# Attention and squared-ReLU FFN on one core: scaling the next pair's q behind the visit's exponentials at the end of a unit

## The chip, the cores and the metric

The kernel runs on one core of one Trainium2 chip. Times are device microseconds of that core, as a median of runs; the profile adds one execution in detail. Lower is better. Engine names: PE is TensorE, DVE is VectorE, ACT is ScalarE, POOL is GpSimd and SP is SyncE, which here only issues DMAs.

## The reference

An attention block with normalized q and k is followed by a feed-forward block, all in float32:

```python
def rmsnorm(x, g):
    return x / np.sqrt(np.mean(x * x, axis=-1, keepdims=True) + 1e-06) * g
# q, k, v: (8, 12, 448, 64); g_q, g_k: (64,)
q_n, k_n = rmsnorm(q, g_q), rmsnorm(k, g_k)
scores = 1 / np.sqrt(64) * np.matmul(q_n, k_n.transpose(0, 1, 3, 2))
scores = scores - scores.max(-1, keepdims=True)
attn = np.exp(scores); attn = attn / (attn.sum(-1, keepdims=True) + 1e-09)
x = np.matmul(attn, v)            # -> (8*448, 12*64) = (3584, 768)
h = np.maximum(x @ w_in, 0)       # w_in: (768, 2048)
out = h * h @ w_out               # w_out: (2048, 768)
```

## The kernel before

**Pairs and visits.** The 96 heads are taken two at a time: 48 pairs, numbered i = 0 to 47, six to a batch element. A pair's q and k are turned so that the head dimension lies on the partitions: two heads of 64 fill 128 partitions, in tiles `qT` and `kT` of 128 x 448. In a visit of pair i its scores are multiplied on TensorE (`score`, L435 and L446), and their exponentials are taken on ACT into tiles `wT` (`weigh`, L454). Between them the attention of the pair before, i - 1, is multiplied (`attend`, with `attend_halves` at L550 and `attend_both` at L571). For i > 24, `whole(i)`, a pair has one visit, `visit_whole`; earlier ones have two. A whole visit goes through three slots of keys: attention of i - 1, scores of i, exponentials of i. At an odd i the PSUM banks of the scores are used in turn, so that the scores of the second slot need a bank which the first slot's exponentials have emptied. At the end of the visit `join_halves` copies two banks on ACT (L561, L562).

**Units and their streams.** The FFN is computed for two batch elements at a time, in four units u = 0 to 3. It is a generator, `ffn(u)`: TensorE multiplies with pre-combined forms of the weights (L986 in unit 0 and L1042 later for the first product, L1251 for the second), and ACT, DVE and POOL move and combine the results. `run(until)` takes steps of this stream up to a point given in costs. Between steps it runs small pieces of work from lists: `tasks`, `pool_tasks`, a `plan` and `transfers`. Twelve pairs' visits are spread over a unit. Where a unit ends (`x == unit`), `drain()` finishes the stream and empties the lists, the next unit's stream is set up, and then the visit follows: no FFN step lies between the drained work and the visit.

**Order.** The order of instructions on every engine is that in which the program issues them, by hand[...]. Nearly all DMAs are issued from SP, in one order too.

**Turning q and k.** For later pairs, `load_blocks` brings q and k in blocks of 32, and `turn_blocks(i, x)` transposes them on DVE (L367). For q (x = 0) it then multiplies `qT` in place on ACT by the 128 factors `g`, which hold g_q * g_k / 8 (L369). Before a whole visit i, tasks for turning k and then q of pair i + 1 are put into `tasks`; most are run between steps of the stream, the rest in `drain()`.

**Other lines named below.** L1039 and L1031 copy a bank of the first product on ACT, and L1027 adds on DVE. L1345 and L1272 add products to the output rows on DVE. L719 is a subtraction that builds a combined form of x (DVE or POOL). L204 and L219 normalize q on POOL; L326 is any DMA that goes through the transfer list: q and k from memory, the normalized q to memory (`q_rows`), and its blocks back. L377 and L384 load v. L892 loads pieces of the first weights (`in_sb`) into a ring, L902 the second weights (`out_sb`), and L1350 stores output rows. `leave(i)` gives up a pair's tiles once its attention is finished.

Of the kernel before, what the change touches and what calls it, by code (L numbers as in the profile page):

```python
# [225 lines left out]
def program(ctx, tc, rows, v, g, wide, ones, moe_w_in, moe_w_out, out, shift):  # L226
# [40 lines left out]
    values, turned, through = {}, {}, {}  # L267
# [9 lines left out]
    def whole(i):  # L277
        return i > 2 * 2 * NPAIR
# [30 lines left out]
    def room_for_blocks(i, x):  # L309
        return rows.room(i)[:, x].rearrange("p g h d -> p (g h d)")[:, ds(i % 2 * S, S)]  # L310
# [17 lines left out]
    def ensure(*key):  # L328

        while any(some[0] == key for some in transfers):  # L330
            follow_transfers(1)
# [32 lines left out]
    def turn_blocks(i, x):  # L364
        ensure("blocks", i, x)
        dst = att.tile([P, S], F32, name="qT" if x == 0 else "kT")
        nc.vector.transpose(dst, room_for_blocks(i, x))  # L367
        if x == 0:
            nc.scalar.mul(dst, dst, g)  # L369
        turned[i, x] = dst  # L370

    def load_v(i):
        b, c = pairs[i]
# [85 lines left out]
    def additions(i):  # L459

        order = [NJ, 2] if i % 2 else [2, NJ]
        for m in [1] + order:
            for e in range(2):
                pool_tasks.append(lambda m=m, e=e: add_up(i, e, m))

    def add_up(i, e, m):
        if m == 1:
            sums[i, e] = new_sum(i)
            left = weights[(i, 0), e]
        else:  # L470
            left = sums[i, e]
        some = ds(i % 2 * LASTS, LASTS) if m == NJ else ds(0, P)
        nc.gpsimd.tensor_tensor(  # L473
            out=sums[i, e][some], in0=left[some], in1=weights[key_of(i, m), e][some], op=ALU.add
        )
        if joint(i) and i % 2 and m == NJ:
            del weights[key_of(i, m), e]
# [217 lines left out]

    def leave(i):
        b, c = pairs[i]
        for x in range(2):
            del turned[i, x]
        del values[i]  # L700
        if b == 1:
            begin_forms(c)
        elif b > 1:
            settle(b, c)
# [16 lines left out]
    def settle(b, c):  # L721

        u = b // 2
        if u - 1 not in through_with and (b % 2 * NPAIR + c) < 8:
            away[b, c] = dram.tile([P, S], F32, name="x_rows", tag="x_rows", bufs=8)
            unsaved[b, c] = xts.pop((b, c))
            later.append([4, lambda: save(b, c)])
        arriving.append([4, (b, c)])
# [5 lines left out]
    def arrive(all_=False):  # L734

        for some in arriving:
            some[0] -= 1
        while arriving and (all_ or arriving[0][0] <= 0):
            here.add(arriving.popleft()[1])
# [101 lines left out]
    def follow_plan(most):  # L841

        while plan and most:
            tiles, x, step = plan[0]
            if tiles > free.get(max(through_with), 0) or not here.issuperset(x):
                break
            plan.popleft()
            if step is not None:
                step()
            most = most - 1 if step else 0  # L850

    def begin_forms(c):

        if c < NK:
            b11, b12, t1 = xts.pop((0, c)), xts.pop((1, c)), new_x()
            less(nc.vector, t1, b12, b11)()
            forms[0, c] = {"11": b11, "T1": t1, "T3": b12}
            return
        c -= NK
        b21, b22, t2, t4 = xts.pop((0, c + NK)), xts.pop((1, c + NK)), new_x(), new_x()  # L860
        some = forms[0, c]
        less(nc.vector, t2, b22, some["T1"])()
        less(nc.gpsimd, some["T3"], b22, some["T3"])()
        less(nc.gpsimd, t4, t2, b21)()
        some.update({"21": b21, "22": b22, "T2": t2, "T4": t4})
# [750 lines left out]
    def run_all():  # L1616
        before = set(held)
        held.clear()
        while tasks or pool_tasks:
            run_tasks(len(tasks) + len(pool_tasks))  # L1620
        if not first:
            follow_transfers(len(transfers))
        held.update(before)

    def drain():
        for _ in stream:
            pass
        while tasks or pool_tasks:
            run_all()
        arrive(True)  # L1630
        while any(some is MARK for some in plan):
            before = len(plan)
            follow_plan(1)
            assert len(plan) < before
# [10 lines left out]
    def load_qk(i):  # L1645
        if i <= last:
            rows.load(i, transfers_of("qk", i))
# [24 lines left out]
    def attend_all(i):  # L1672
        slots = range(NJ + 1)
        attend(i, slots)
        add_weights(i, slots)
        forget(i, slots)
        take_sums(i)
        invert(i)
        finish(i)
# [90 lines left out]
            tasks.append(lambda: load_blocks(i, 1))  # L1770

    def visit_whole(i):
        late = [some for some in tasks if getattr(some, "args", None) == (i,)]
        for some in late:
            tasks.remove(some)
        run_all()
        if shift:
            attend_all(i - 1)
            if i <= last:
                weigh_slots(i, 1)  # L1780
        else:
            if i % 2 == 0:
                both_denominators(i - 2)
            for n in range(NJ):
                attend(i - 1, (n,))
                forget(i - 1, (n,))
                if i <= last:
                    score(i, n)
                    weigh(i, n)
                while n == 1 and i % 2 == 0 and late:  # L1790
                    late.pop(0)()
            if i % 2:
                attend(i - 1, (NJ,))
                forget(i - 1, (NJ,))
            join_halves(i - 1)
            if i % 2 == 0:
                tasks.append(lambda: invert_both(i - 2))
                if i <= last:
                    score(i, NJ)
                    weigh(i, NJ)  # L1800
            if i <= last:
                additions(i)
        tasks.extendleft(reversed(late))
        if late:
            tasks.extendleft([gap] * 3)
        if shift or i % 2:
            prepare(i + 3)
        else:
            tasks.append(lambda: tasks.append(lambda: prepare(i + 3, 0)))
        if i <= last:  # L1810
            tasks.appendleft(lambda: load_v(i))
# [7 lines left out]
    with tc.manual_schedule(engines=ENGINES):  # L1819
        if shift:  # L1820
            rows.scale(0, 1, nc.gpsimd)
        turn(0, 1)
        turn(0, 0)
        for x in range(2):
            rows.normalize_first(1, x, new_acc()[:, 0 : 4 * P])
        if shift:
            rows.scale(1, 1, nc.gpsimd)
        for i in range(len(pairs) + 1):
            for n in range(1 if whole(i) else VISITS):
                at = i * VISITS + n - VISITS - unit  # L1830
                if at < 0:
                    visit_alone(i, n)
                    continue
                u, x = divmod(at, unit)
                if x == 0:
                    u, x = u - 1, unit
                run(place(u, x - (1 if whole(i - 1) else 0.5)))
                if i < last:
                    if whole(i) and not shift:
                        tasks.append(partial(lambda i: turn_blocks(i + 1, 1), i))  # L1840
                        tasks.append(partial(lambda i: turn_blocks(i + 1, 0), i))
                        tasks.append(partial(lambda i: load_qk(i + 4), i))
                    else:
                        for some in (1, 0) if whole(i) else (1 - n,):
                            turn_among(i + 1, some)
                        if n or whole(i):
                            tasks.append(lambda i=i: load_qk(i + 4))
                    if n and first and x > 1 and not shift:
                        denominators(i - 1)
                run(place(u, x))  # L1850
                if x == unit:
                    drain()
                    stream, spent, first = ffn(u + 1), 0, u < 0
                    if shift:
                        run(COST if first else LATER)
                    elif first:
                        run(COST_IN + 1)
                slowly = x < unit
                if whole(i):
                    visit_whole(i)  # L1860
                else:
                    visit_among(i, n)
        run(LATER)
        drain()
        assert not transfers
        for _ in ffn(B // 2 - 1):
            follow_loads()
            follow_plan(1)
# [29 lines left out]
```

## Time and profile before

| | |
|---|---|
| median of 3 runs | 1392.92 us (1391.83 to 1393.26) |
| profiled execution: its own time | 1394.38 us |
| profiled execution: span from first to last instruction | 1392.6 us |
| busy share of the span: PE, DVE, ACT, POOL | 98%, 58%, 44%, 57% |
| PE's granted clock, mean | 0.998 of full speed |
| DMA moved | 233.36 MB, mean 168 GB/s |
| L369, the multiply of q: count, mean | 34, 665 ns |
| L454, the exponentials into wT: count, mean | 288, 631 ns |

The page gives for each engine the time in which it was busy and, for each group of instructions, the idle time in front of them with what ended it. In the timeline a row is a run of like instructions: start and duration in us, engine, line, operation, output<-input, the count, and in brackets the idle time before it and its releaser. PEld is the loading of weights, which overlaps the matmuls; SPq are the DMA issues of SP. The chain of waits starts from the last instruction and follows back what released each step.

### The profile page before, as it was taken

Reading aid. Unit: us, or ns where it says so; the run is one execution under the profiler, and the core shown is the slowest. Engines: PE = TensorE matmul, PEld = TensorE weight load, DVE = VectorE, ACT = ScalarE, POOL = GpSimd, SP = SyncE. Lnnn points to the kernel's source line nnn. Section 1 sums busy time; section 2 is a strip of 40 time slices with the busy share of each in tenths; the row PEclk is TensorE's granted clock in tenths of the full one; section 3 lists DMA queues with packets and bytes.
Section 4 is the critical chain, followed back from the end, with each engine's and each line's share of the span. In section 5 each row is a group of like instructions: output and inputs, shape, how many; then the busy total and the mean of one; then the engine's idle time right before and its main releaser. Section 6 shows DMA issues by size and latency. Waiting matters only on the chain.

```text
span 1392.6 us, 19474 instructions
## 1 busy us (share of the span) xinstructions
PE 1363.3 (98%) x6320; PEld 845.7 (61%) x6320; DVE 807.2 (58%) x1635; ACT 608.3 (44%) x1118; POOL 789.6 (57%) x794
## 2 busy tenths in 40 slices
PE   7999999999999999999999999999999999999997
PEld 3333444444444466676758586676768677868684
DVE  4786545867758755555556755455546642445444
ACT  6885477757666244353434244442434032202020
POOL 5668664746656868576667877566745630303030
PEclk9999999999999999999999999999999999999999
DMA  5566746968769875664739475755527442424223
GB/s 147 149 168 169 203 117 159 264 179 219 233 155 284 231 215 162 187 173 141 204 86 279 140 225 149 211 153 176 146 86 239 142 165 103 135 90 149 78 90 100
DMA packets 385588, 233.36 MB, mean 168 GB/s; under 512 B 272452, under 2 KB 354244, under 8 KB 381380
## 3 DMA queue, kind: packets, MB, share of 16 engines
q1 hardware_dynamic: 385184, 231.95, 57.7%
q8 instruction: 52, 0.85, 0.3%
q14 instruction: 60, 0.49, 0.1%
q10 hardware_dynamic: 292, 0.07, 0.0%
HBM read 174.59 MB, written 57.34 MB: 167 GB/s over the span
## 4 chain that ended last, share of the span: by engine, by line
PE 81%; POOL 4%; DVE 4%; DMA 3%; issue 3%; SPq 2%; ACT 2%; POOLq 0%; ACTq 0%; DVEq 0%
PE bank L1251 30%; PE bank L1042 20%; PE bank L986 8%; PE bank L446 5%; PE bank L536 5%; PE bank L550 4%; PE bank L435 4%; PE bank L1165 2%; POOL sum L473 2%; PE bank L585 1%; DMA qk<-in_k_dram 1%; PE bank L611 1%; SPq L326 1%; SPq L318 1%; PE bank L571 1%
## 5 line engine op out<-in xcount | busy, mean ns | idle before, releaser
L1042 PE MATMUL bank<-xT,in_sb 128*128 128x224 f32 x1344 | 289.3, 354 | 2.9 <-ACT part L1031 2.3
L1251 PE MATMUL bank<-out_sb,hid 128*128 128x384 f32 x768 | 272.5, 488 | 2.2 <-POOL out_sb L1514 1.4
L1345 DVE TENSOR_TENSOR acc<-acc,bank 128x384 f32<-128x384 f32 x312 | 166.6, 548 | 164.6 <-PE bank L1251 138.1
L1042 PEld LDWEIGHTS bank<-xT,in_sb 128*128 128x128 f32 x1344 | 252.6, 190 | 15.0 <-ACT wT L454 5.6
L454 ACT ACTIVATE wT<-bank,rr 128x448 f32<-128x448 f32 x288 | 163.5, 631 | 155.1 <-PE bank L435 92.7
L1251 PE MATMUL bank<-out_sb,sums 128*128 128x384 f32 x576 | 207.2, 490 | 1.3 <-DVE acc L1345 0.9
L1251 PEld LDWEIGHTS bank<-out_sb,hid 128*128 128x128 f32 x768 | 144.7, 190 | 104.5 <-issue 5.6
L204 POOL TENSOR_TENSOR rr<-ms,minus_half 128x8 f32<-128x8 f32 (+1 forms) x96 | 146.0, 1521 | 73.7 <-DVE ms L197 63.8
L1251 PEld LDWEIGHTS bank<-out_sb,sums 128*128 128x128 f32 x576 | 107.7, 190 | 86.3 <-issue 4.3
L1027 DVE TENSOR_TENSOR hid<-hid,bank 128x224 f32<-128x224 f32 x312 | 111.0, 383 | 83.9 <-PE bank L1042 79.1
L986 PE MATMUL bank<-xT,in_sb 128*128 128x448 f32 x336 | 131.9, 546 | 0.1
L473 POOL TENSOR_TENSOR sum<-sum,wT 128x448 f32<-128x448 f32 (+1 forms) x96 | 110.6, 1173 | 8.1 <-ACT wT L454 6.6
L986 PEld LDWEIGHTS bank<-xT,in_sb 128*128 128x128 f32 x336 | 62.1, 190 | 69.0 <-issue 60.2
L446 PE MATMUL bank<-qT,kT 64*128 64x448 f32 (+1 forms) x492 | 100.5, 571 | 1.9 <-DVE qT L409 1.1
L473 POOL TENSOR_TENSOR sum<-wT 128x448 f32<-128x448 f32 x48 | 55.8, 1183 | 69.8 <-ACT wT L454 69.8
L1099 ACT ACTIVATE hid<-hid 128x448 f32<-128x448 f32 x96 | 55.0, 573 | 66.7 <-DVE hid L1027 48.5
L435 PE MATMUL bank<-qT,kT 64*64 64x448 f32 x552 | 77.0, 547 | 1.9 <-ACT wT L454 1.9
L1042 PE MATMUL bank<-more,in_sb 128*128 128x224 f32 x288 | 76.2, 357 | 1.4 <-DVE hid L1037 1.4
L550 PE MATMUL bank<-wT,vt 64*64 64x448 f32 x576 | 74.3, 548 | 0.0
L1039 ACT COPY hid<-bank 128x448 f32<-128x448 f32 x24 | 12.8, 532 | 137.3 <-PE bank L1042 137.3
L369 ACT ACTIVATE qT<-qT,g 128x448 f32<-128x448 f32 x34 | 22.6, 665 | 113.7 <-DVE qT L367 113.7
L446 PEld LDWEIGHTS bank<-qT,kT 64*128 64x128 f32 (+1 forms) x492 | 34.9, 166 | 60.4 <-issue 36.8
(140 smaller groups left out, 2059.1 us busy)
## 6 DMA issues: line engine op xcount, KB each, us to landing
out_sb<-out_forms SPq DMA_DIRECT2D x24, 1536.0 KB, 9.9
in_sb<-in_deep SPq DMA_DIRECT2D x64, 384.0 KB, 4.2
in_sb<-in_deep SPq DMA_DIRECT2D x80, 256.0 KB, 4.1
words<-in_moe_w_in_dram SPq DMA_DIRECT2D x32, 384.0 KB, 3.8
words<-in_moe_w_out_dram SPq DMA_DIRECT2D x32, 384.0 KB, 3.6
out_forms<-out_sb SPq DMA_DIRECT2D x8, 1536.0 KB, 7.5
qk<-in_q_dram SPq DMA_DIRECT2D x96, 96.0 KB, 2.6
qk<-in_k_dram SPq DMA_DIRECT2D x96, 96.0 KB, 2.7
```

The lines of the kernel that those rows point to most:

```text
L204: self.nc.gpsimd.tensor_tensor(out=self.rr[i][:, x, 0 : self.count(i)], in0=ms, in1=self.minus_half.to_broadcast(list(ms.shape)), op=ALU.pow,)
L435: nc.tensor.matmul(sc[ds(half * D, D)], lhsT=turned[i, 1][ds(e * D, D), ds(m * P + half * D, D)], rhs=turned[i, 0][ds(e * D, D), :], start ...
L446: nc.tensor.matmul(sc[some], lhsT=turned[p, 1][r, keys], rhs=turned[p, 0][r, :], start=True, stop=True,)
L454: nc.scalar.activation(new_weights((i, m), e), sc, AF.Exp, scale=rows.rr[i][:, 1, 2 * m + e : 2 * m + e + 1],)
L473: nc.gpsimd.tensor_tensor(out=sums[i, e][some], in0=left[some], in1=weights[key_of(i, m), e][some], op=ALU.add)
L536: nc.tensor.matmul(values_bank(i)[ds(e * D, D), :], lhsT=lasts[i % 2][mine, e, :] if m == NJ else values[i][:, m, e, :], rhs=weights[key_o ...
L550: nc.tensor.matmul(bank[ds(e * D, D), :], lhsT=values[i][keys, n, e, :], rhs=weights[(i, n), e][keys], start=n == 0, stop=n == NJ - 1 and ...
L986: nc.tensor.matmul(ps, lhsT=w_sb[:, IN.index(left), c, :], rhs=forms[u, c][right], start=first and c == 0, stop=c == NK - 1, skip_group_ch ...
L1027: nc.vector.tensor_tensor(out=quarter(name, n), in0=quarter(base, n), in1=ps, op=ALU.add)
L1042: nc.tensor.matmul(ps, lhsT=left, rhs=right, start=start, stop=stop, skip_group_check=True)
L1251: nc.tensor.matmul(ps, lhsT=extra[left][:, t] if tt == NT else lefts[left][:, t, ts(tt, P)], rhs=w_sb[t][:, OUT.index(right), :], start=fi ...
L1345: nc.vector.tensor_tensor(out=acc, in0=acc, in1=ps, op=ALU.add)
```

## The change

At the end of a unit before a whole visit, the multiply by `g` is not issued with the transpose but kept in a list, and issued at the end of `visit_whole`, behind that visit's exponentials and the copies of `join_halves`. Elsewhere, `turn_blocks` issues it at once, as before. `leave` also issues what is in the list. The flag `closing` is set just before `drain()` and cleared at the end of the visit.

```diff
@@ -365,9 +365,18 @@
         ensure("blocks", i, x)
         dst = att.tile([P, S], F32, name="qT" if x == 0 else "kT")
         nc.vector.transpose(dst, room_for_blocks(i, x))
+        turned[i, x] = dst
         if x == 0:
+            to_scale.append(dst)
+            if not closing:
+                scale_turned()
+
+    def scale_turned():
+        while to_scale:
+            dst = to_scale.popleft()
             nc.scalar.mul(dst, dst, g)
-        turned[i, x] = dst
+
+    to_scale, closing = deque(), False
 
     def load_v(i):
         b, c = pairs[i]
@@ -695,6 +704,7 @@
 
     def leave(i):
         b, c = pairs[i]
+        scale_turned()
         for x in range(2):
             del turned[i, x]
         del values[i]
@@ -1770,6 +1780,7 @@
             tasks.append(lambda: load_blocks(i, 1))
 
     def visit_whole(i):
+        nonlocal closing
         late = [some for some in tasks if getattr(some, "args", None) == (i,)]
         for some in late:
             tasks.remove(some)
@@ -1800,6 +1811,8 @@
                     weigh(i, NJ)
             if i <= last:
                 additions(i)
+        closing = False
+        scale_turned()
         tasks.extendleft(reversed(late))
         if late:
             tasks.extendleft([gap] * 3)
@@ -1849,6 +1862,7 @@
                         denominators(i - 1)
                 run(place(u, x))
                 if x == unit:
+                    closing = whole(i)
                     drain()
                     stream, spent, first = ffn(u + 1), 0, u < 0
                     if shift:
```

## The prediction

> **What bounds the kernel now.** I read the page first, then the timeline around the two places where the diff can act, then the chain of waits, then the SP queue's own waits.
>
> ```profile
> PE 1363.3 (98%) x6320; PEld 845.7 (61%) x6320; DVE 807.2 (58%) x1635; ACT 608.3 (44%) x1118; POOL 789.6 (57%) x794
> ...
> L369 ACT ACTIVATE qT<-qT,g 128x448 f32<-128x448 f32 x34 | 22.6, 665 | 113.7 <-DVE qT L367 113.7
> ```
>
> TensorE is busy 98% of the span, so only what makes it wait or run badly can be won. The scaling of q (L369) costs 0.67 us each and 22.6 us in all on ACT, which is idle for more than half of the span. Its 113.7 us of idle time are a queue standing still for a transpose on DVE. That matters only where TensorE needs something from ACT meanwhile.
>
> A unit ends where the stream of an FFN runs out and a visit follows at once with nothing between. The new flag can be set at two such ends only: visits 25 and 37, the ends of units 0 and 1 (visit 13 is not "whole"). The timeline of the first, start and duration in us, then engine, line and tiles, idle time and releaser in brackets:
>
> ```profile
> 486.33 0.98 PE L550 MATMUL bank<-wT,vt 64*64 64x448 f32 x8
> ...
> 487.13 0.93 PE L435 MATMUL bank<-qT,kT 64*64 64x448 f32 x8
> ...
> 489.56 0.60 DVE L367 STREAM_TRANSPOSE qT<-qk 128x448 f32<-128x448 f32 x1
> ...
> 490.20 0.67 ACT L369 ACTIVATE qT<-qT,g 128x448 f32<-128x448 f32 x1 [6.06 <-DVE qT L367]
> ...
> 490.77 2.44 ACT L454 ACTIVATE wT<-bank,rr 128x448 f32<-128x448 f32 x4
> ...
> 491.44 0.59 PE L435 MATMUL bank<-qT,kT 64*64 64x448 f32 x2 [1.89 <-ACT wT L454]
> ...
> 496.29 0.65 PE L1042 MATMUL bank<-xT,in_sb 128*128 128x224 f32 x2
> ```
>
> The first scores are written at 487.13 + 0.93 = 488.06. Their exponentials start at 490.77, because L369 stands in front of them on ACT and waits for a transpose that ends at 490.16. TensorE needs the bank that the first exponential empties, and stops for 1.89 us. From the first attention matmul to the first FFN matmul (L1042) it takes 496.29 - 486.33 = 9.96 us.
>
> The second end:
>
> ```profile
> 799.46 0.60 DVE L367 STREAM_TRANSPOSE qT<-qk 128x448 f32<-128x448 f32 x1
> ...
> 799.99 1.44 DVE L1345 TENSOR_TENSOR acc<-acc,bank 128x384 f32<-128x384 f32 x3
> 800.09 0.67 ACT L369 ACTIVATE qT<-qT,g 128x448 f32<-128x448 f32 x1 [4.43 <-DVE qT L367]
> 800.23 0.98 PE L550 MATMUL bank<-wT,vt 64*64 64x448 f32 x8
> ...
> 802.00 1.16 ACT L454 ACTIVATE wT<-bank,rr 128x448 f32<-128x448 f32 x2 [1.24 <-PE bank L435]
> ...
> 805.87 0.65 PE L1042 MATMUL bank<-xT,in_sb 128*128 128x224 f32 x2
> ```
>
> Here the multiply is done at 800.76, ACT then idles 1.24 us for scores, and the same work takes 805.87 - 800.23 = 5.64 us. This is the undisturbed visit. Also, the q transpose precedes three L1345 additions of the stream's last products, so it is issued while the stream runs, before the flag is set. At the first end it follows the last L1345 (487.24 to 488.25) and two L719 steps, so it comes out of the draining with the flag set. **The change therefore acts once, at visit 25.**
>
> What follows that visit is in the SP queue's timeline and the chain of waits. The queue's own waits add that SP waited for L1042 on TensorE for 1.4 us in front of 498.48 and for 1.2 us in front of 502.77.
>
> ```profile
> 498.48 0.34 SPq L892 DMA_DIRECT2D in_sb<-in_deep  x1
> ...
> 499.82 2.02 SPq L902 DMA_DIRECT2D out_sb<-out_forms  x2
> ...
> 502.77 1.11 SPq L892 DMA_DIRECT2D in_sb<-in_deep  x2
> ```
>
> ```profile
> 515.38 0.34 SPq L892
> ...
> 521.61 1.81 DMA q_rows<-qk
> ...
> 528.56 3.62 DMA in_sb<-in_deep
> ...
> 532.32 1.37 PE bank L1042 x6
> ```
>
> At 532.32 TensorE waits 0.57 us for a piece of weights (256 KB, issued at 528.56, landed at 532.18). Its issue comes last in a chain of SP issues without a gap, apart from 0.7 us for a landing at 523.42. SP in turn ran behind the transfers: DMA engines are 93% busy from 500 to 520 us at 309 GB/s, and the two 1536 KB loads of L902 took 11.7 us to land.
>
> [...] exponentials with operands ready at 488.06 start 2.71 us later, behind a multiply for another pair. [...] from 490.20 to 490.77 is 0.57 us, an overlap of 0.10. [...] eight 64*64 matmuls take 0.93 us undisturbed. [...]
>
> **The change, part by part.** Nothing is added or removed: 34 multiplies before and after. One ACT instruction moves behind six exponentials and two copies (L561, L562). No DMA moves in program order; SP and POOL keep their queues. The Python flag and list cost nothing on the chip.
>
> *The visit.* With nothing before them, the exponentials start at about 488.10 instead of 490.77 (2.67 us). The other 1.65 us of the difference between 9.96 and 5.64 come from the stall's aftermath: from 491.44 to 496.3 the score and attention matmuls run two at a time instead of four groups deep, as the two heads have come apart. I take the undisturbed visit for the new one: the FFN begins at 486.33 + 5.64 = 491.97, **4.32 us** earlier. ACT has been free since 484.13, and the attention matmuls of pair 24 release the weight buffers as at 800 us, so I see no second wait behind the first.
>
> *The multiply in its new place.* Its transpose is over at 490.16 and ACT reaches it about 0.42 us (the pitch of two copies) after L562 begins. At the second end L562 begins 0.60 us after the first L1042 matmul, so here near 492.57, and the multiply at 492.99. It takes a pitch of 0.57, to 493.56. Behind it stands L1039, the first copy out of the FFN's banks, which would start 1.43 us after the first L1042 matmul, at 493.40: 0.16 us late. TensorE waits for that copy (0.21 us of weight-load idle), so it costs 0.16 us, at most 0.57. The scaled q is needed one visit later, some 14 us on: no cost. From both sides: 0 if the next wait swallows it, 0.57 if not.
>
> *What is late next.* TensorE then reaches the matmul of 532.32 at 531.75 - 4.32 + 0.16 = 527.6, if the load is there. The load depends on SP. SP up to 496.44 is fixed by POOL's scaling (ends 490.68), a store of q that must land, and eight issues behind it; none of these moves, apart from 0.1 us. Then two waits for TensorE go away. The 1.4 us in front of 498.48 vanish: L892 at about 497.0, L902 at 498.35, **1.5 us earlier**. The 1.2 us in front of 502.77 vanish too, [...] from 505.8 to 510.9 it is held in one issue. So the burst of transfers, same bytes at the same rate, ends 1.5 us earlier. Another 0.2 to 0.3 us come at 514.35 to 515.38, where SP now waits for TensorE with the engines half idle. The load lands at about 532.18 - 1.75 = 530.4, and TensorE, there at 527.6, waits 2.9 us instead of 0.57. The bounds: 1.5 us, the burst alone; and about 3.0, if SP's way from L902 to this load shrinks from 28.1 us to the 26.5 that it takes at the second end (809.57 to 836.06).
>
> *Sum.* Gained 4.32; late copy -0.16, swallowed by the longer wait; taken back by the weights about 2.4. Net **-1.8 us** at 532 us. From there SP, DMA and the engines are all some 1.8 us early together, and no other matmul waits idle for a DMA up to the end, so I let it stand. The profiled execution took 1394.38 us, 1.8 around its span of 1392.6, and lies 1.46 above the median of 1392.92. Its forecast is 1392.6, and the median's 1392.92 - 1.8 = **1391.1 us**.
>
> About 0.2% (2.8 us) is what a measurement of this kernel can tell from no change. My likeliest case lies inside.
>
> **The rivals.** *The weights do not hold it back* (chance 0.20): the burst empties sooner and the load lands before 527.6, or nearly so. Then 3 to 4.3 us remain, 1388.6 to 1389.9. For it: the 1.6 us by which the second end is quicker over the same way. Against it: SP's fixed start at 496.4. *The change doesn't act* (0.07): the transpose was issued before the flag was set, or a second wait holds the exponentials. Then 1392.9. Against it: the order on DVE told above, and ACT's idle 6.06 us. *The early burst backfires* (0.06): L902's 3 MB start 1.5 us sooner, run into the last small transfers of q and v (issued 492.69 to 496), and stretch SP's way to the load at 528.56. This is slower than before from the point at which the load lands after 532.2, and by over 0.2% only after 535, so the way must grow from 28.1 to over 32 us; I price it at 1396. The spread of 1.6 us seen between the ends speaks against it. The remaining 0.67 is the likeliest case, at 1.5 to 2.7 us, with a small part above the bound.
>
> **How the numbers follow.** Faster by over 0.2%: 0.20 and some 0.05 from the upper edge of the likeliest case, 0.25. Slower: 0.06. Within: 0.69. The range goes from just beyond the full gain, 1388.5, to no gain, 1393.0. The likeliest case alone would be 1390.2 to 1391.4.
>
> **What would show it.** Right, if around 488 us ACT's first exponentials follow the scores directly, L369 stands after L562, the way to the first L1042 matmul is about 5.6 us, and the wait for in_sb at about 530 us has grown to 2 to 3 us. L369 stays in front of the exponentials at the second end. Wrong, if that wait stays under 1 us (then the gain is whole), if TensorE finds another wait in the visit, or if the span from 540 us on is not the old one moved by one amount.

## The result, and the profile after

The changed kernel takes **1396.42 us** (median of 20 runs, 1392.92 to 1397.79), against 1393.60 us (20 runs, 1390.45 to 1397.79) for the kernel before on the same chip. The measured ratio, which is not just the quotient of the two medians, is 1.0017, with a 95% interval of 1.0011 to 1.0023: a small loss instead of the small gain that was forecast, and outside the range. The profiled execution took 1396.53 us, 1.8 around its span of 1394.7; it is compared below with the profiled execution of before (1394.38 and 1392.6).

Eight to ten lines lie between the numbers of the two programs: L369 is now L377, L435 is L444, L454 is L463, L550 is L559, L562 is L571, L892 is L902, L902 is L912, L1039 is L1049, L1042 is L1052, L1251 is L1261, L1350 is L1360. L367 stays. In the experiments inserted lines move some numbers once more, so that L1261 is L1267 or L1265.

The page's line of busy times and its row of the FFN's first product (busy us, mean ns of one, then idle time and what ended most of it), and below them the same row of the kernel before:

```profile
PE 1364.3 (98%) x6320; PEld 847.5 (61%) x6320; DVE 806.2 (58%) x1635; ACT 608.1 (44%) x1118; POOL 789.2 (57%) x794
...
L1052 PE MATMUL bank<-xT,in_sb 128*128 128x224 f32 x1344 | 290.6, 355 | 7.2 <-DMA in_sb<-in_deep 4.9
```

```profile
L1042 PE MATMUL bank<-xT,in_sb 128*128 128x224 f32 x1344 | 289.3, 354 | 2.9 <-ACT part L1031 2.3
```

Two things can be read from it already. Nearly five of the 7.2 us of idle time before these matmuls are now one wait for weights; and TensorE, with the same 6320 matmuls, was *busy* 1.0 us longer (1363.3 before). So some of the same matmuls took longer; the table by stretches below shows at which clock.

The timeline of the changed visit, at the end of unit 0 (start, duration, engine, line and tiles, idle time and releaser in brackets):

```profile
486.14 0.98 PE L559 MATMUL bank<-wT,vt 64*64 64x448 f32 x8
...
488.00 1.16 ACT L463 ACTIVATE wT<-bank,rr 128x448 f32<-128x448 f32 x2 [4.04 <-PE bank L444]
...
491.84 0.65 PE L1052 MATMUL bank<-xT,in_sb 128*128 128x224 f32 x2
...
492.44 0.55 ACT L571 COPY xT<-bank 128x448 f32<-128x448 f32 x1
...
492.86 0.70 ACT L377 ACTIVATE qT<-qT,g 128x448 f32<-128x448 f32 x1
...
493.43 0.55 ACT L1049 COPY hid<-bank 128x448 f32<-128x448 f32 x1
```

The exponentials now wait for the scores and for nothing else, the multiply stands behind the second copy, and the way from the first attention matmul to the first FFN matmul is 491.84 - 486.14 = 5.70 us, where it was 9.96. The visit does what was intended of it.

SP's timeline behind that visit:

```profile
496.27 2.27 SPq L902 DMA_DIRECT2D in_sb<-in_deep  x2
498.64 0.85 SPq L1360 DMA_DIRECT2D out_dram<-acc  x2
499.55 1.86 SPq L912 DMA_DIRECT2D out_sb<-out_forms  x2
501.50 1.30 SPq L902 DMA_DIRECT2D in_sb<-in_deep  x2
```

The second of the two loads at 496.27 no longer waits for TensorE, but the first issue alone took 1.80 us, so the two 1536 KB loads (L912) are issued at 499.55, only 0.27 us earlier than before (499.82).

The chain of waits and then TensorE's timeline, where the FFN needs the second pieces of weights:

```profile
528.61 3.60 DMA in_sb<-in_deep
532.21 0.14 issue
532.34 2.58 PE bank L1052 x6
```

```profile
526.94 0.54 PE L1052 MATMUL bank<-xT,in_sb 128*128 128x224 f32 x2
532.34 2.58 PE L1052 MATMUL bank<-xT,in_sb 128*128 128x224 f32 x6 [4.86 <-DMA in_sb<-in_deep]
534.71 2.77 PE L1261 MATMUL bank<-out_sb,hid 128*128 128x384 f32 x4
537.27 0.74 PE L1052 MATMUL bank<-more,in_sb 128*128 128x224 f32 x2
...
538.23 2.74 PE L1261 MATMUL bank<-out_sb,hid 128*128 128x384 f32 x8
```

The same place in the kernel before, and then the first attention matmuls of the next visit, before and after:

```profile
532.32 1.37 PE L1042 MATMUL bank<-xT,in_sb 128*128 128x224 f32 x6 [0.57 <-DMA in_sb<-in_deep]
533.52 1.45 PE L1251 MATMUL bank<-out_sb,hid 128*128 128x384 f32 x4
...
535.57 2.75 PE L1251 MATMUL bank<-out_sb,hid 128*128 128x384 f32 x8
...
543.40 0.98 PE L550 MATMUL bank<-wT,vt 64*64 64x448 f32 x8
```

```profile
546.06 0.98 PE L559 MATMUL bank<-wT,vt 64*64 64x448 f32 x8
```

The piece lands at 532.21, when it landed before (532.18). TensorE, there 4.3 us sooner, waits 4.86 us instead of 0.57, and the gain is gone. But then the six matmuls that took 1.37 us take 2.58, and the four of L1261 take 2.77 instead of 1.45. What that is stands in the table by stretches (length, busy us and count of PE, PEld, DVE, ACT and POOL, then the granted clock PEclk, DMA share, GB/s), first of the kernel before, then of the changed one:

```profile
532.00:534.00 2.00, 1.69 (x8) 1.58 (x9) 0.28 (x1) 1.94 (x5) 1.14 (x1) 1.00 0.94 303
534.00:537.00 3.00, 3.00 (x13) 2.07 (x12) 2.19 (x6) 1.38 (x4) 2.56 (x3) 1.00 1.01 383
```

```profile
532.00:534.00 2.00, 1.66 (x5) 1.54 (x6) 0.00 (x0) 0.00 (x0) 2.00 (x3) 0.50 0.92 282
534.00:537.00 3.00, 3.00 (x7) 1.99 (x6) 0.68 (x2) 0.00 (x0) 0.06 (x1) 0.50 1.03 391
```

TensorE's **clock is halved** after the wait. The trace's clock record has one stretch at 0.50 here, 6.83 us long, from about 530.8 to 537.7. From 532.34 on that is some 5.3 us at half speed, half of which is lost: about 2.7 us. Before, the way from the first of these matmuls to the eight of L1261 took 535.57 - 532.32 = 3.25 us; now it takes 538.23 - 532.34 = 5.89, 2.64 more. At the next visit the changed kernel is 2.66 us behind (546.06 against 543.40 for the first attention matmul), at the second end 2.70 (802.93 against 800.23), and at the end of the span 2.1.

### The profile page after: what moved, and what is told of

It is laid out like the page before. It is cut to its first block, busy times and chain, and to the rows that moved or that the text cites. A ratio compares the mean times of both kernels' runs of the same rounds, so it can differ in the third digit from the quotient of the medians.

```text
span 1394.7 us, 19474 instructions
## 1 busy us (share of the span) xinstructions
PE 1364.3 (98%) x6320; PEld 847.5 (61%) x6320; DVE 806.2 (58%) x1635; ACT 608.1 (44%) x1118; POOL 789.2 (57%) x794
## 4 chain that ended last, share of the span: by engine, by line
PE 78%; POOL 6%; issue 4%; DMA 3%; DVE 3%; SPq 3%; ACT 2%; POOLq 0%; DVEq 0%; ACTq 0%
PE bank L1261 32%; PE bank L1052 21%; PE bank L996 5%; PE bank L559 4%; PE bank L444 4%; PE bank L455 4%; PE bank L545 3%; PE bank L1175 2%; POOL sum L482 2%; DMA words<-in_moe_w_out_dram 1%; PE bank L620 1%; POOL rr L204 1%; SPq L326 1%; SPq L318 1%; PE bank L580 1%
## 5 line engine op out<-in xcount | busy, mean ns | idle before, releaser
L1052 PE MATMUL bank<-xT,in_sb 128*128 128x224 f32 x1344 | 290.6, 355 | 7.2 <-DMA in_sb<-in_deep 4.9
L1261 PE MATMUL bank<-out_sb,hid 128*128 128x384 f32 x768 | 273.8, 490 | 2.2 <-POOL out_sb L1524 1.4
L1052 PEld LDWEIGHTS bank<-xT,in_sb 128*128 128x128 f32 x1344 | 253.3, 191 | 19.6 <-ACT wT L463 5.6
L463 ACT ACTIVATE wT<-bank,rr 128x448 f32<-128x448 f32 x288 | 163.4, 631 | 159.5 <-PE bank L444 97.0
L1261 PEld LDWEIGHTS bank<-out_sb,hid 128*128 128x128 f32 x768 | 145.3, 191 | 104.9 <-issue 6.2
L1261 PE MATMUL bank<-out_sb,sums 128*128 128x384 f32 x576 | 207.1, 490 | 1.1 <-DVE acc L1355 0.6
L1261 PEld LDWEIGHTS bank<-out_sb,sums 128*128 128x128 f32 x576 | 107.6, 190 | 86.0 <-DVE acc L1355 4.4
L1052 PE MATMUL bank<-more,in_sb 128*128 128x224 f32 x288 | 76.4, 358 | 1.4 <-DVE hid L1047 1.4
L444 PE MATMUL bank<-qT,kT 64*64 64x448 f32 x552 | 74.5, 541 | 0.0
L559 PE MATMUL bank<-wT,vt 64*64 64x448 f32 x576 | 73.0, 545 | 0.0
L1049 ACT COPY hid<-bank 128x448 f32<-128x448 f32 x24 | 12.8, 533 | 136.9 <-PE bank L1052 136.9
L1213 POOL TENSOR_TENSOR wT<-wT 128x256 f32<-128x256 f32 x16 | 11.5, 730 | 105.1 <-DMA wT<-rests 104.4
```

The source lines that it names most:

```text
L444: nc.tensor.matmul(sc[ds(half * D, D)], lhsT=turned[i, 1][ds(e * D, D), ds(m * P + half * D, D)], rhs=turned[i, 0][ds(e * D, D), :], start ...
L463: nc.scalar.activation(new_weights((i, m), e), sc, AF.Exp, scale=rows.rr[i][:, 1, 2 * m + e : 2 * m + e + 1],)
L559: nc.tensor.matmul(bank[ds(e * D, D), :], lhsT=values[i][keys, n, e, :], rhs=weights[(i, n), e][keys], start=n == 0, stop=n == NJ - 1 and ...
L1052: nc.tensor.matmul(ps, lhsT=left, rhs=right, start=start, stop=stop, skip_group_check=True)
L1261: nc.tensor.matmul(ps, lhsT=extra[left][:, t] if tt == NT else lefts[left][:, t, ts(tt, P)], rhs=w_sb[t][:, OUT.index(right), :], start=fi ...
```

## The experiments

Theory: the loss is the halved clock, which follows TensorE's idling for the weights; the wait itself only takes back what the visit gained. Rivals: the transfers are disturbed by the earlier FFN; or the order of loads, not the multiply, is where any gain lies. Each kernel was timed beside the kernel before. `busy`, `pieces`, `early` and `early_old` share one set of runs of it (median 1393.39, 46 runs), the other three another (1393.08, 33 runs). The ratios are again not just quotients of the medians.

| kernel | median us (runs) | ratio to before, 95% interval |
|---|---|---|
| `busy`: changed, six spare matmuls in the wait | 1393.51 (14) | 1.0001, 0.9993 to 1.0009 |
| `busy3`: changed, three spare matmuls | 1393.43 (12) | 0.9997, 0.9985 to 1.0008 |
| `filled_old`: before, three spare matmuls in the visit's stall | 1393.28 (12) | 0.9996, 0.9988 to 1.0005 |
| `pieces`: changed, pieces of weights ahead of q and k | 1390.02 (8) | 0.9972, 0.9962 to 0.9982 |
| `pieces_old`: before, the same order | 1393.23 (13) | 0.9996, 0.9988 to 1.0005 |
| `early`: changed, the 1536 KB loads earlier | 1391.55 (22) | 0.9986, 0.9980 to 0.9993 |
| `early_old`: before, the same loads earlier | 1393.01 (14) | 0.9997, 0.9989 to 1.0005 |

### Keep TensorE busy while it waits

```diff
+                if (u, blk, k) == (1, 0, 6):
+                    for _ in range(6):
+                        multiply(
+                            banks[3][:, 0:S], ident, forms[u, 0][right][:, 0:S],
+                            start=True, stop=True,
+                        )
```

> The changed kernel with six spare matmuls (128x448, into an unused bank, some 4.5 us) just ahead of the matmul that waits 4.86 us for its piece of weights in the first block of unit 1. Theory (the idle TensorE has its clock halved, which costs some 2.6 us on top of the wait): the wait is filled, the granted clock stays full from 527 to 540 us, and the time falls from 1396.4 by 2.4 to 2.8 us to that of before, 1393.6 to 1394.0. Rival (the slow matmuls after the wait have another cause, the DMA traffic for one, or the loss lies elsewhere): the clock is halved at 532 us all the same, and the time stays at 1396 or above.

Measured: 1393.51 us. TensorE's timeline in this kernel:

```profile
526.49 4.67 PE L1052 MATMUL bank<-xT,wide 128*128 128x448 f32 x12
531.00 1.30 PE L1052 MATMUL bank<-xT,in_sb 128*128 128x224 f32 x6
532.13 1.45 PE L1267 MATMUL bank<-out_sb,hid 128*128 128x384 f32 x4
```

Twelve records for six spare multiplies: in these traces each appears as a pair (the three of `busy3` below as six). They do nothing useful, but the six matmuls behind them take 1.30 us and the four of L1267 1.45, and the granted clock is 1.00 from 524 to 537 us. The weights did land a little earlier here, 0.7 us counted from the visit (530.64 - 485.26 = 45.38 us against 532.21 - 486.14 = 46.07), but that is not where the time was won: from the six matmuls to the next visit it takes 542.01 - 531.00 = 11.01 us, against 546.06 - 532.34 = 13.72. Work that is thrown away won 2.9 us in the median (1396.42 to 1393.51), or 2.7 when each is counted from the median of before beside it. **The loss is the clock.** And without that loss the changed kernel only equals the one before: the wait takes back all that the visit gains.

With three spare multiplies instead of six:

> The changed kernel with three spare matmuls of 128x448 (about 2.3 us of TensorE, results not used) ahead of the FFN's wait for its second pieces of in weights in the first block of unit 1, so that the wait of 4.9 us is cut to about 2.5. Theory (an idle stretch of TensorE is followed by a halved clock, and its length goes with that of the idle stretch): 3.4 us at half clock in place of 6.8, so a loss of about 1.5 us in place of 2.9, and a time between the kernel with six spare matmuls (1393.5) and the changed kernel (1396.4): about 1394.9. If 2.5 us idle bring no halved clock: 1393.5. If they bring the full 6.8 us: 1396.4.

```profile
528.01 2.42 PE L1052 MATMUL bank<-xT,wide 128*128 128x448 f32 x6
531.16 1.37 PE L1052 MATMUL bank<-xT,in_sb 128*128 128x224 f32 x6 [0.74 <-DMA in_sb<-in_deep]
```

Measured: 1393.43 us, as with six, and a granted clock of 1.00 from 524 to 546 us. It did not test what it was for: here the load landed 1.9 us earlier against the visit (531.02 - 486.84 = 44.18 us), and the idle time left was 0.74 us, not 2.5. What an idle time of 2.5 us would bring stays open.

### Fill the stall of the visit in the kernel before

The forecast put 1.65 us of the visit's 9.96 down to the two heads' having come apart. The clock offers another reading: the record of before has 3.41 us at half clock, from 492.2 to 495.6; it begins 0.7 us after the stall of 1.89 us is over. Three spare multiplies in that stall, in `score`:

```diff
+                for _ in range(3 if (i, m, e) == (2 * unit // VISITS + 1, 1, 1) else 0):
+                    nc.tensor.matmul(
+                        banks[7][:, 0:S], lhsT=ident, rhs=turned[i, 0], start=True, stop=True
+                    )
```

> The kernel before, with three spare matmuls of 128x448 (about 2.2 us of TensorE, results not used) in the stall of the visit at the end of unit 0, so that TensorE is idle there for less than half a microsecond. The exponentials come as late as before. Theory (of the visit's 9.96 us, 1.89 are the stall and most of the rest over 5.7 is a TensorE clock that is halved for 3.4 us after the stall): no halved clock from 492 to 496, and the FFN begins 8.1 to 8.6 us after the visit's first attention matmul; the end of the kernel is then within 1 us of before, as the FFN waits about 2 us for its second pieces of weights. Rival (the prediction's reading: the rest is the two heads' having come apart): the clock plays no part, and the FFN still begins 9.9 us or more after that matmul.

```profile
486.07 0.98 PE L554 MATMUL bank<-wT,vt 64*64 64x448 f32 x8
...
489.22 2.52 PE L435 MATMUL bank<-qT,wide 128*128 128x448 f32 x6
...
491.68 0.59 PE L439 MATMUL bank<-qT,kT 64*64 64x448 f32 x2
...
494.83 0.65 PE L1046 MATMUL bank<-xT,in_sb 128*128 128x224 f32 x2
```

The stretch from 490 to 496 us (columns as in the table by stretches above; the clock is third from the end) in the kernel before and then here:

```profile
490.00:496.00 6.00, 4.56 (x28) 1.69 (x28) 0.17 (x1) 3.91 (x7) 5.92 (x7) 0.72 0.36 74
```

```profile
490.00:496.00 6.00, 6.00 (x39) 2.84 (x38) 0.05 (x1) 5.07 (x9) 5.92 (x7) 1.00 0.40 82
```

The first true score comes at 491.68, no earlier than before (491.44); the scores still stand two at a time. Yet the FFN begins 494.83 - 486.07 = 8.76 us after the first attention matmul, with the clock at 1.00 from 490 to 496 (0.72 before). That is 0.2 us above the expected 8.1 to 8.6, because the spare matmuls run 0.5 us too long: the score comes 5.61 us after the first attention matmul instead of 5.11. Behind the score the way to the FFN is 494.83 - 491.68 = 3.15 us instead of 496.29 - 491.44 = 4.85. So the rival falls: of the visit's 9.96 us, the halved clock is 1.70.

The kernel's time is that of before, as expected, though not for the reason given: the FFN's wait for its second pieces was 0.53 us, not 2. A likelier reason, not tested, is that the halved clock comes only in some executions of the kernel before, as below under `pieces_old`.

### Bring the weights earlier, by the order on SP

In the first block of unit 1 the transfers of q and k are held back until three steps of the first product have issued their pieces of `in_sb`. The 1536 KB loads stay where they are. The list's definition and the same condition in `run_all` are not printed here.

```diff
+        if (u, blk) == (1, 0):
+            pieces_first.append(True)
...
+                if (u, blk, k) == (1, 0, 2):
+                    pieces_first.clear()
...
-        follow_transfers(to_send)
+        follow_transfers(0 if pieces_first else to_send)
...
```

> The changed kernel in which, in the first block of unit 1, the loads and stores of q and k wait in their list until the step that issues the late piece of weights is done; the 1536 KB loads stay where they are. Theory (the order on SP's queue decides, with SP held until the second large load lands at 514): the piece is issued at about 515 to 518 us instead of 528.6 and landed by 522, no wait at 528 us, 1389.0 to 1389.6. Rival (the rate of the DMA engines decides): the piece is issued early but lands after 530 us, and the time is 1394 to 1396.

```profile
526.28 1.20 PE L1052 MATMUL bank<-more,in_sb 128*128 128x224 f32 x4
527.31 1.68 PE L1052 MATMUL bank<-xT,in_sb 128*128 128x224 f32 x8
528.83 1.45 PE L1265 MATMUL bank<-out_sb,hid 128*128 128x384 f32 x4
```

The eight matmuls are two and the six that waited in the rows above: no idle time is left in front of them, and the granted clock is 1.00 from 484 to 546 us. The late piece was the ninth issue of `in_sb` in this stretch; the ninth is now issued at 514.39 instead of 528.61. Measured: 1390.02 us, 0.28% under the kernel before, and 0.4 us short of the expected 1389.0 to 1389.6. It is the fastest of the versions tried.

The same order without the moved multiply:

> The kernel before (multiply in front of the exponentials), with the order of the next unit's loads changed: its q and k transfers are held back until the first pieces of its in weights have been issued. Theory (the order pays because it takes away a wait that the earlier FFN would run into): without the moved multiply the visit at the end of unit 0 still takes some 9.96 us, and only the wait of 0.57 us before the FFN's second pieces of weights can go, so 1392.6 to 1393.1 us against 1393.4 for the kernel before. Rival (the order by itself is the gain, and the moved multiply adds nothing): 1390 us, as with both changes.

Measured: 1393.23 us, a shade above what the theory gave and nowhere near the 1390 of the rival. The order alone is worth nothing that can be measured, the multiply alone costs 2.8 us, and both together win 3.4 (differences of medians). Its profile adds a finding. TensorE stalls as in before, and the clock is **not** halved:

```profile
485.98 0.98 PE L550 MATMUL bank<-wT,vt 64*64 64x448 f32 x8
...
491.09 0.59 PE L435 MATMUL bank<-qT,kT 64*64 64x448 f32 x2 [1.89 <-ACT wT L454]
...
494.24 0.65 PE L1042 MATMUL bank<-xT,in_sb 128*128 128x224 f32 x2
```

```profile
490.00:496.00 6.00, 4.91 (x37) 2.94 (x38) 0.62 (x1) 5.27 (x10) 5.92 (x7) 1.00 0.40 82
```

The visit takes 8.26 us here. With the same stall of 1.89 us and a halved clock it took 9.96. So a stall of that length is followed by a halved clock in one execution and not in another, and the difference, 1.70 us, is about what the forecast gave to the two heads (1.65).

### Bring the weights earlier, by the large loads

The loads of `out_sb` at the end of unit 0 are put ahead of v and the first pieces.

```diff
-        later.append([4, lambda: [load_out(n + 2) for n in ns]])
+        if (u, blk) == (0, NBLK - 1):
+            later.appendleft([1, lambda: [load_out(n + 2) for n in ns]])
+        else:
+            later.append([4, lambda: [load_out(n + 2) for n in ns]])
```

> The changed kernel with the two 1536 KB loads of second weights, at the end of unit 0 alone, issued ahead of v and of the first pieces of unit 1 instead of behind them, some 5 us earlier. Theory (SP's queue, held by these two loads, brings the piece of weights too late): SP reaches the piece 3 to 5 us earlier, the wait of 4.86 us and the halved clock are gone, and the whole 4.4 us of the visit stay: 1389.0 to 1389.6. Rival (the order of the small transfers, not these loads, sets when the piece lands): the wait stays above 3 us, the time within 1 us of 1396.4.

```profile
494.92 0.90 SPq L912 DMA_DIRECT2D out_sb<-out_forms  x2
498.02 5.30 SPq L902 DMA_DIRECT2D in_sb<-in_deep  x2
```

```profile
529.53 1.37 PE L1052 MATMUL bank<-xT,in_sb 128*128 128x224 f32 x6 [0.76 <-DMA in_sb<-in_deep]
```

The right way and 2 us short of the forecast. The loads start 4.6 us sooner than in the changed kernel, but the piece lands only 2.8 sooner (525.83 + 3.57 = 529.40), for SP's issues of the two pieces behind the loads now take 5.30 us, where in front of the loads they took 2.27 (at 496.27 in the changed kernel). The wait falls to 0.76 us, the granted clock is 1.00 from 484 to 546 us, and the kernel wins 0.14% over before.

> The kernel before with the same two loads issued earlier. Theory: there the piece is waited for only 0.57 us, so 0.5 to 0.7 us are won, 1392.9 to 1393.1, and the stall in the visit with its halved clock stays. Rival (the earlier loads are a gain by themselves, whatever the multiply does): 3 us or more are won here too, 1390 or below.

Measured: 1393.01 us, as expected: the kernel before has nothing to gain from earlier loads, since the work behind its stalled visit reaches the piece late enough.

## Why the prediction was wrong

Two terms of its sum failed. *What is late next* had the weights land 1.5 to 1.75 us earlier; they landed when they did before, and the wait of 4.86 us instead of 2.9 took back the whole gain. And the sum put at nothing what that wait does to the clock behind it, which cost 2.64 us and turned no gain into a loss.

**The change acts once: right.** At the second end the multiply stands in front of the exponentials as before (802.79 against 804.70).

**The visit: right in size, wrong in one cause.** 5.70 us measured, 5.64 forecast. But the 1.65 us for "the two heads have come apart" are the halved clock, as `filled_old` and `pieces_old` show. This is where the missing term comes from: the evidence that a stall can slow the matmuls *after* it lay in the trace of before, as a PEclk of 0.72 from 490 to 496, and was explained by something else. So no such term was written down for the wait of 2.9 us that the forecast itself placed at 530 us. It also makes the gain depend on the execution: against a visit of 8.26 us, as in `pieces_old`, the changed one wins 2.56 us and not 4.26, so the forecast took for the median a gain that only executions with the halved clock have.

**The multiply in its new place: right.** The first copy behind it starts 493.43 - 491.84 = 1.59 us after the first FFN matmul instead of 1.43: 0.16 us late, as forecast, and swallowed by the wait for the weights.

**What is late next: wrong, by its term of 1.5 us.** "L902 at 498.35, 1.5 us earlier" was measured at 499.55, 0.27 us earlier, since the issue ahead of it took 1.80 us and not the 0.6 assumed. The further "0.2 to 0.3" did not come either, and the DMA engines that it calls half idle had a busy share of 0.82 from 514.35 to 515.38 in before. That the piece follows these loads was sound for a shift of this size: in `filled_old` they were issued at 498.37, and the piece landed at 527.03 + 3.67 = 530.70, 1.5 us before the 532.18 of the kernel before. In the changed kernel it landed at 532.21. So TensorE waited 4.86 us and not 2.9, and at 532.34 nothing was won.

Why that one issue took 1.80 us no experiment tried, but the traces point to one cause. A 16 KB packet of the instruction queue is under way from 496.37 to 497.68 us, and the issue (496.27 to 498.07) ends 0.39 us behind it. In `busy`, `busy3` and `pieces` such a packet also overlaps an issue of `in_sb` here; these issues took 1.15, 1.67 and 0.93 us and ended 0.38 to 0.39 us behind the packet. Of the 52 such packets in the changed kernel's trace, 29 end while SP is issuing, and 25 of those issues end 0.30 to 0.43 us behind the packet. In the kernel before, the packet came later, at 502.06 to 503.01. So the issue probably stood behind that packet, but this is read from the traces and not shown by a test.

Two more of the forecast's readings of SP were off, without weight for the result. The 28.1 us "from L902 to this load" end at the issue ahead of it (527.92); to the load itself they are 28.7, and 27.1 at the second end, with the same difference of 1.6. And the one issue that is held lasts from 505.7 to 510.2; the stretch to 510.9 is two issues.

**"From there all some 1.8 us early together": wrong, by a missing term.** The step assumed that TensorE works after a wait as before it. The clock of 0.50 cost 2.64 us. In the profiled executions the corrected sum is -4.27 (TensorE's arrival at the matmul), +4.29 (wait of 4.86 instead of 0.57), +2.64 (clock): +2.66 us, which is what the next visit shows.

**The rivals.** *The weights do not hold it back* fell with the wait of 4.86 us, *the change doesn't act* with the visit of 5.70 us. *The early burst backfires* had the right sign and the wrong place: it needed a piece that lands later, and some 4 us more on SP's way from the loads to that piece; counted from the first of the loads, the way went from 28.7 us (499.82 to 528.56) to 29.1 (499.55 to 528.61). The piece came when it used to; TensorE took it at a granted clock of 0.50.

**How often.** The mean granted clock of the timed runs, in steps of 0.001, is in line with this beyond the profiled executions: it was 0.996 in 11 of 20 runs of the changed kernel (median 1396.6 us) and never 0.999, while `busy` had 0.999 in 12 of 14 and the kernel before, in the runs beside it, in 20 of 46. The three runs of the changed kernel at 0.998 include two of 1392.9 and 1393.2. The mean is a rough sign, since every trace also ends with 2.1 to 5.2 us at half clock inside the span.

## What to carry to other kernels

Moving work off the path makes the engine arrive earlier at the next thing that it needs; look up when that lands, and move it too, or the gain turns into a wait (here 4.86 us in place of 0.57). A new idle stretch of a few microseconds on TensorE is priced as the stretch plus a possible time at half clock behind it, which may turn no change into a loss (here 1.70 us behind 1.89 idle, 2.64 behind 4.86, and nothing behind the 1.89 of `pieces_old`). When equal matmuls take longer in one place than in another (here six in 2.58 us at a granted clock of 0.50, and in 1.37 at 1.00), look at the granted clock of that stretch before you think of an explanation from the program's order.

## What the runs showed of the hardware

The halved clock came in stretches of 3.413 us (before, `early_old`, after a stall of 1.9 us) and 6.827 us (changed, from about 3.4 us into a wait of 4.86 us on): one and two units of the same length. In the clock records of before and of the changed kernel every stretch but the last is a whole number of these units. In before, 477.866 us at full clock, 3.413 at half and 894.292 at full are 140, 1 and 262 of them; in the changed kernel, 515.413 at full, 6.827 at half and 853.332 at full are 151, 2 and 250. I read from this that the units run on through the kernel, and take each trace's own changes of clock for their bounds. The idle time of TensorE can then be counted by unit (us from the span's start):

| trace | TensorE idle | idle in each unit | clock in the unit behind it |
|---|---|---|---|
| before | 489.55 to 491.44 | 1.89 (488.77 to 492.18) | half |
| `early_old` | 491.46 to 493.36 | 1.90 (491.17 to 494.59) | half |
| `pieces_old` | 489.20 to 491.09 | 0.74 (486.53 to 489.94), 1.15 (489.94 to 493.36) | full, full |
| changed | 527.48 to 532.34 | 3.36 (527.43 to 530.84), 1.50 (530.84 to 534.25) | half, half |

By this count before and `pieces_old` differ in where the stall of 1.89 us lies: in one within a unit, in the other across a bound, as 0.74 and 1.15. It would also say why the halving in before starts only at 492.18: two matmuls of L435 take 0.59 us at 491.44, right behind the stall, and 0.96 at 492.32. Over the nine traces, leaving out the first 20 us and the end, a halved unit follows the four units of the table with 1.50 us or more and no other; the most idle time without one is 1.17 us (at the end of before, left out here, 1.40 in the unit from 1383.06 to 1386.48). Where between the two the line lies, and whether it is the same at half clock, no run shows, and no run was built to move a stall against the units. Counted by the stall alone, 1.9 us were followed by half clock in two profiled executions of three: before and `early_old`, not `pieces_old`.
